# A fused linear-attention and SwiGLU kernel on one core: another order of work for its first five tiles

## The chip, the cores and the metric

The kernel runs on one core of a Trainium2 chip. The core has five engines that run side by side, each through its own list of instructions in order: TensorE (PE, matrix products; its weight loads are shown as PEld), VectorE (DVE), ScalarE (ACT), GpSimd (POOL) and SyncE (SP, which here only issues transfers). They wait for each other through semaphores. The metric is the device time of one execution in microseconds (us), the median over runs.

## The reference

One input x of 2048 rows and 512 columns is normalised and goes through linear attention with 32 heads of 16, and through a SwiGLU block with an inner width of 1792; both results are added to x. Weights and data are bfloat16.

```python
def _A_ref(x, wqkv, wo):
    qkv = (lambda x, *d: x.transpose(*d))((x @ wqkv).reshape(B, S, 3, H, Dh), 2, 0, 3, 1, 4)
    q, k, v = qkv[0], qkv[1], qkv[2]
    phi = lambda t: jnp.where(t > 0, t + 1, jnp.exp(t)) + 1e-6
    pq, pk = phi(q), phi(k)
    kv = jnp.einsum("bhsd,bhse->bhde", pk, v)
    z = jnp.einsum("bhsd->bhd", pk)
    num = jnp.einsum("bhqd,bhde->bhqe", pq, kv)
    den = jnp.einsum("bhqd,bhd->bhq", pq, z)[..., None] + 1e-6
    o = num / den
    return (lambda x, *d: x.transpose(*d))(o, 0, 2, 1, 3).reshape(B, S, D) @ wo

def _B_ref(x, w_gate, w_up, w_down):
    g = _silu(x @ w_gate)
    u = x @ w_up
    return (g * u) @ w_down

x = A_x
xn = _layernorm(x, axis=-1)
return x + _A_ref(xn, A_wqkv, A_wo) + _B_ref(xn, B_w_gate, B_w_up, B_w_down)
```

## The kernel before

The 2048 rows are 16 tiles of 128. Phase 1 runs over the tiles: layernorm, the products K = xn wk and Q = xn wq, the feature map phi, and a running product GT = xn^T phi(K), which stays in four PSUM banks (4 to 7) over all tiles (`gtacc`, line 516). V is never formed: after the last tile GT is multiplied by the V weights, masked per head and multiplied by wo. Phase 2 is the SwiGLU block, 56 steps of a gate product and an up product (`ffn`, line 692), with the attention's division and the output tiles placed between its steps. Only phase 1 is touched.

The order is written out by hand. A small recorder (`_Prog`) appends each operation to the list of its engine and derives the waits from the tiles that it reads and writes; what stands first in the text stands first on its engine. An operation that waits holds up everything behind it on that engine. Nothing is reordered later.

The steps of a tile t, with the names used below:

- `bns` (line 295) and `agg` (298), on VectorE: mean and variance. `rstd_pow` (313): variance plus 1e-5, on GpSimd or, for tiles 3 and 5, on VectorE, then the power -0.5 on GpSimd, which gives rstd.
- Tiles 0, 1 and 2 take a short way that doesn't wait for rstd: `xc_half` (346, VectorE) subtracts the mean in two halves, `tp_first` (356) transposes a half on PE (line 361) into bank 4 to 7 and copies it to SBUF on ScalarE (370), `proj_first` (395) multiplies two of the four blocks (half h) by the K or Q weights (line 400). rstd enters afterwards as the scale of ScalarE's `first_ek`, `first_pk`, `first_eq`, `first_pq` (exp of K, the positive part of K, exp of Q, Q).
- From tile 3 on: `xn_dve` (301, VectorE) writes the normalised tile, `transpose_dma` (374) issues a DMA transpose of it on SP's queue (line 377) into xnT, `kproj` and `qproj` (415, 418; matmuls at line 386) multiply it, `exp_k` and `exp_q` (421, 427) run on ScalarE; `exp_q` also copies Q.
- Features of K: `clip` (437, VectorE: min with 1, plus 1e-6), then `maxadd` (446) or, for tiles 1 and 2, `first_feat` (486) on VectorE; for tile 0 `feat_pool` (479) on GpSimd. The result is pk. `zsum` (504, GpSimd) adds pk up for the denominator; `feat_k` (493) bundles clip, the zsum of three tiles before, and maxadd.
- `gtacc(t)` needs xn and pk of the tile.

K of tile t goes to bank 2 (t mod 2), Q to the bank after it, so tile t + 2 waits until ScalarE and VectorE have read tile t's. At the start `fill` (264) runs matmuls on constants into bank 3.

Loads are issued first: x of tiles 0 to 5 one by one, the K weights and the Q weights in blocks, on SP's and ScalarE's queues; then x of tiles 6 to 9 and 10 to 13 on SP's queue. x of tiles 14 and 15 is loaded from ScalarE's queue, at the place in ScalarE's order where line 605 stands. Behind the loads SP's queue holds the DMA transposes in the order of the text. From t = 4 the loop at line 637 takes over; the dictionaries `STAT`, `XN0` and `XN` (632 to 635) say in which step the statistics and the normalisation of a later tile are done.

On PE the order of the groups before is: 8 long fills; transposes of tile 0 with 2 and 3 short fills behind its halves; K 0 first half; transposes of tile 1; K 0 second half; K 1; first halves of Q 0 and Q 1; transposes of tile 2; second halves of Q 0 and Q 1; K 2; GT 0; Q 2; GT 1; GT 2; K 3; Q 3; then K 4, Q 4, GT 3, K 5, and so on.

Of the kernel before, what the change touches and what calls it, by code (L numbers as in the profile page):

```python
# [10 lines left out]
P = 128  # L11
# [97 lines left out]
def bass_parallel_sum__linear_attn_block__swiglu_ffn__prompt_kernel(  # L109
# [16 lines left out]
    with contextlib.ExitStack() as es:  # L126
# [61 lines left out]
        def bk(i):  # L188
            return ("bank", i)
# [118 lines left out]
                r=[("x", t), ("mv", t), ("rstd", t)], w=[("xn", t)],  # L308
            )

        VD = (3, 5)

        def rstd_pow(t):
            eng, h = ("dve", dve) if t in VD else ("pool", pool)
            K.op(
                eng,
                lambda: h.tensor_scalar(
                    out=vpe[:, t:t + 1], in0=mv[:, t, 1:2], scalar1=1e-5, scalar2=None, op0=ALU.add,
                ),
                r=[("mv", t)], w=[("vpe", t)],  # L320
            )
            K.op(
                "pool",
                lambda: pool.tensor_tensor(out=rstd[:, t:t + 1], in0=vpe[:, t:t + 1], in1=nhalf[:, :], op=ALU.pow),
                r=[("vpe", t), ("nhalf",)], w=[("rstd", t)],
            )
# [82 lines left out]
        def kb(t):  # L409
            return 2 * (t % 2)  # L410
# [16 lines left out]
        def exp_q(t):  # L427
            K.op(
                "act", lambda: act.activation(eq[:, t, :], banks[qb(t)], ACT.Exp),
                r=[bk(qb(t))], w=[("eq", t)],  # L430
            )
            K.op(
                "act", lambda: act.activation(pkq[:, t, 1, :], banks[qb(t)], ACT.Copy),
                r=[bk(qb(t))], w=[("pq", t)],
            )

        def clip(e, res):
            K.op(
                "dve",
                lambda: dve.tensor_scalar(  # L440
                    out=e, in0=e, scalar1=1.0, scalar2=1e-6, op0=ALU.min, op1=ALU.add,
                ),
                r=[res], w=[res],
            )

        def maxadd(dst, src, e, r, w):
            K.op(
                "dve",
                lambda: dve.scalar_tensor_tensor(  # L449
                    out=dst, in0=src, scalar=0.0, in1=e, op0=ALU.max, op1=ALU.add,  # L450
                ),
                r=r, w=w,
            )
# [32 lines left out]
        def first_feat(t):  # L486
# [3 lines left out]
                r=[("kpos", t), ("ek", t)], w=[("pk", t)],  # L490
            )

        def feat_k(t):
            e = t % NE
            clip(ek[:, e, :], ("ek", e))
            if t >= 3:
                zsum(t - 3, e)
            maxadd(pkq[:, t, 0, :], banks[kb(t)], ek[:, e, :], [bk(kb(t)), ("ek", e)], [("pk", t)])

        def feat_q(t):  # L500
            clip(eq[:, t, :], ("eq", t))
# [2 lines left out]
        def zsum(t, e):  # L504
            pk = pkq[:, t, 0, :]
            after = [] if e is None else [("ek", e)]
            if t == 0:
                K.op("pool", lambda: pool.tensor_copy(zacc[:, :], pk), r=[("pk", t)] + after, w=[("zacc",)])
            else:
                K.op(  # L510
                    "pool",
                    lambda: pool.tensor_tensor(out=zacc[:, :], in0=zacc[:, :], in1=pk, op=ALU.add),  # L512
                    r=[("pk", t), ("zacc",)] + after, w=[("zacc",)],
                )
# [14 lines left out]
        def stat(t):  # L529
            bns(t)  # L530
            agg(t)
            rstd_pow(t)

        def xn(t):
            xn_dve(t)
            if t >= 3:
                transpose_dma(t)

        bns(0)
        agg(0)  # L540
        rstd_pow(0)
        xc_half(0, 0)
        xc_half(0, 1)
        bns(1)
        agg(1)
        rstd_pow(1)
        xc_half(1, 0)
        xc_half(1, 1)
        bns(2)
        agg(2)  # L550
        rstd_pow(2)
        xn_dve(0)
        xc_half(2, 0)
        xc_half(2, 1)

        fill(8, 512)
        tp_first(0, 0, 4)
        fill(2, P)
        tp_first(0, 1, 5)
        fill(3, P)  # L560
        proj_first(0, "wk", 0)
        tp_first(1, 0, 6)
        tp_first(1, 1, 7)
        proj_first(0, "wk", 1)
        first_ek(0)
        first_pk(0)
        proj_first(1, "wk", 0)
        proj_first(1, "wk", 1)
        first_ek(1)
        proj_first(0, "wq", 0)  # L570
        proj_first(1, "wq", 0)
        tp_first(2, 0, 4)
        tp_first(2, 1, 5)
        proj_first(0, "wq", 1)
        proj_first(1, "wq", 1)
        clip(ek[:, 0, :], ("ek", 0))
        feat_pool(0)
        bns(3)
        agg(3)
        rstd_pow(3)  # L580
        bns(4)
        clip(ek[:, 1, :], ("ek", 1))
        first_pk(1)
        first_eq(0)
        first_pq(0)
        proj_first(2, "wk", 0)
        proj_first(2, "wk", 1)
        gtacc(0)
        xn_dve(2)
        xn(3)  # L590
        agg(4)
        first_feat(1)
        rstd_pow(4)
        xn_dve(1)
        first_ek(2)
        first_pk(2)
        first_eq(1)
        first_pq(1)
        clip(ek[:, 2, :], ("ek", 2))
        xn(4)  # L600
        proj_first(2, "wq", 0)
        proj_first(2, "wq", 1)
        gtacc(1)
        first_eq(2)
        xload("act", act, 14, 2)
        first_pq(2)
        first_feat(2)
        bns(5)
        agg(5)
        rstd_pow(5)  # L610
        gtacc(2)
        bns(6)
        agg(6)
        rstd_pow(6)
        xn(5)
        kproj(3)
        exp_k(3)
        qproj(3)
        exp_q(3)
        bns(7)  # L620
        clip(ek[:, 0, :], ("ek", 0))
        xn(6)
        agg(7)
        rstd_pow(7)
        zsum(0, 0)
        maxadd(pkq[:, 3, 0, :], banks[kb(3)], ek[:, 0, :], [bk(kb(3)), ("ek", 0)], [("pk", 3)])
        bns(8)
        xn(7)
        agg(8)
        rstd_pow(8)  # L630

        STAT = {4: (9,), 5: (10,), 6: (11,), 7: (12,), 8: (13, 14), 9: (15,)}
        XN0 = {5: (8,), 6: (9,), 7: (10,), 8: (11,), 9: (12, 13), 10: (14,)}
        XN1 = {}
        XN = {10: (15,)}

        for t in range(4, NT):
            kproj(t)
            exp_k(t)
            qproj(t)  # L640
            exp_q(t)
            for i in XN0.get(t, ()):
                xn(i)
            feat_k(t)
            for i in XN1.get(t, ()):
                xn(i)
            for i in STAT.get(t, ()):
                stat(i)
            for i in XN.get(t, ()):
                xn(i)  # L650
            if t in (7, 8, 9):
                transpose_dma(t - 7)
            if t == 10:
                whalf("wg", wg_sb, B_w_gate, 0)
                whalf("wu", wu_sb, B_w_up, 0)
                wqkv_load("sp", sp, "wv", 2, 0, 4)
                wload("sp", sp, "wo", wo_sb, A_wo)
                whalf("wg", wg_sb, B_w_gate, 1)
            if t == 12:
                masks()  # L660
            if t >= 12:
                gtacc(t - 2)
            elif t < 11:
                gtacc(t - 1)
# [298 lines left out]
```

## Time and profile before

| what | value |
|---|---|
| median of 3 runs | 211.75 us (211.73 to 212.23) |
| span of the profiled execution, first to last instruction | 210.8 us |
| granted TensorE clock | 1.000 |
| DMA moved | 16.71 MB |
| HBM read, written | 9.70 MB, 2.10 MB |

The times of the profile lie inside the span and are counted from its first instruction; the median of the runs also has what lies around it. In the timeline a line gives the start, the length from the first start to the last end, the engine, the source line, the operation and its tiles, a count, and in brackets the idle time before it with what ended it. Matmuls overlap, so the lengths of neighbouring groups overlap as well; the distance of their starts is the measure. The lists of groups by line show these mean durations, which the prediction uses: 0.69 us for `bns` (line 296), 0.18 for `agg` (299), 0.48 for `xn_dve` (304), 0.28 for an `xc_half` (349), 0.69 for `maxadd` from PSUM (449), 0.67 for `first_feat` (489), 0.28 to 0.29 for `clip` (440), 0.60 for exp of K (423) and of Q (429), 0.70 for `first_ek` (457), 0.61 for the power on GpSimd (324), 1.15 for an addition on GpSimd (482 and 512).

### The profile page before, as it was taken

Reading aid. Unit: us, or ns where it says so; the run is one execution under the profiler, and the core shown is the slowest. Engines: PE = TensorE matmul, PEld = TensorE weight load, DVE = VectorE, ACT = ScalarE, POOL = GpSimd, SP = SyncE. Lnnn points to the kernel's source line nnn. Section 1 sums busy time; section 2 is a strip of 40 time slices with the busy share of each in tenths; the row PEclk is TensorE's granted clock in tenths of the full one; section 3 lists DMA queues with packets and bytes.
Section 4 is the critical chain, followed back from the end, with each engine's and each line's share of the span. In section 5 each row is a group of like instructions: output and inputs, shape, how many; then the busy total and the mean of one; then the engine's idle time right before and its main releaser. Section 6 shows DMA issues by size and latency. Waiting matters only on the chain.

```text
span 210.8 us, 2758 instructions
## 1 busy us (share of the span) xinstructions
PE 206.5 (98%) x972; PEld 95.8 (45%) x991; DVE 119.7 (57%) x245; ACT 69.8 (33%) x122; POOL 74.4 (35%) x95
## 2 busy tenths in 40 slices
PE   8999999999999999999999999999999999999996
PEld 3444444445444444444444444444444444444455
DVE  4899889335364775546274746365556535374121
ACT  3797666666543331203122312213031213121000
POOL 3647987659032444222140432230424132221200
DMA  6773244794793011110101110102021010110201
GB/s 205 228 214 78 51 100 101 219 369 167 197 357 67 0 26 27 46 25 28 50 2 50 24 28 25 50 0 50 3 50 25 25 25 30 49 27 25 51 28 50
DMA packets 29455, 16.71 MB, mean 79 GB/s; under 512 B 20224, under 2 KB 29056, under 8 KB 29440
## 3 DMA queue, kind: packets, MB, share of 16 engines
q1 hardware_dynamic: 28304, 15.34, 26.4%
q10 hardware_dynamic: 1136, 1.18, 1.8%
q8 instruction: 8, 0.13, 0.2%
q14 instruction: 7, 0.06, 0.1%
HBM read 9.70 MB, written 2.10 MB: 56 GB/s over the span
## 4 chain that ended last, share of the span: by engine, by line
PE 95%; DMA 3%; issue 1%; ACTq 0%; ACT 0%; DVE 0%
PE psum L683 46%; PE psum L866 23%; PE psum L386 11%; PE psum L520 7%; PE psum L855 7%; DMA wqkv_sb<-in_A_wqkv_dram 3%; PE psum L400 2%; PE psum L781 0%; PE psum L804 0%; ACT L232 0%; ACTq L209 0%; DVE out_sb L879 0%; ACTq L202 0%; PE psum L361 0%
## 5 line engine op out<-in xcount | busy, mean ns | idle before, releaser
L698 ACT ACTIVATE sg<-psum 128x512 bf16<-128x512 f32 x56 | 33.4, 598 | 106.8 <-PE psum L683 106.0
L683 PE MATMUL psum<-xnT,wu_sb 128*128 128x512 bf16 x222 | 57.4, 379 | 0.1
L683 PE MATMUL psum<-xnT,wg_sb 128*128 128x512 bf16 x217 | 56.0, 379 | 0.4
L813 POOL TENSOR_TENSOR prod<-pkq,zb 128x512 f32<-128x512 bf16 x16 | 18.6, 1160 | 57.9 <-DVE pkq L449 57.9
L683 PEld LDWEIGHTS psum<-xnT,wu_sb 128*128 128x128 bf16 x224 | 21.9, 98 | 26.4
L683 PEld LDWEIGHTS psum<-xnT,wg_sb 128*128 128x128 bf16 x224 | 21.9, 98 | 26.2
L879 DVE TENSOR_TENSOR out_sb<-psum,x_sb 128x512 bf16<-128x512 f32 (+1 forms) x17 | 11.2, 660 | 35.6 <-PE psum L866 35.6
L837 POOL TENSOR_TENSOR pqn<-pkq,rden 128x512 bf16<-128x512 bf16 x16 | 16.9, 1055 | 36.5 <-DVE rden L831 36.5
L704 DVE TENSOR_TENSOR pkq<-psum,sg 128x512 bf16<-128x512 f32 x28 | 19.1, 687 | 18.6 <-PE psum L683 14.1
L704 DVE TENSOR_TENSOR xn_sb<-psum,sg 128x512 bf16<-128x512 f32 x28 | 18.8, 671 | 14.5 <-PE psum L683 13.0
L866 PE MATMUL psum<-wd_sb,xn_sb 128*128 128x512 bf16 (+1 forms) x124 | 25.6, 355 | 0.1
L866 PE MATMUL psum<-wd_sb,pkq 128*128 128x512 bf16 x110 | 25.4, 379 | 0.1
L386 PE MATMUL psum<-wqkv_sb,xnT 128*128 128x512 bf16 x102 | 24.2, 379 | 0.1
L512 POOL TENSOR_TENSOR zacc<-zacc,pkq 128x512 f32<-128x512 f32 x15 | 17.3, 1154 | 5.0 <-DVE ek L440 4.6
L866 PEld LDWEIGHTS psum<-wd_sb,xn_sb 128*128 128x128 bf16 x126 | 12.3, 98 | 11.9
L866 PEld LDWEIGHTS psum<-wd_sb,pkq 128*128 128x128 bf16 x112 | 11.0, 98 | 13.2
L855 PE MATMUL psum<-m_sb,eq 128*128 128x512 bf16 (+1 forms) x66 | 16.2, 366 | 0.1
L520 PE MATMUL psum<-pkq,xn_sb 128*128 128x512 bf16 x63 | 15.8, 379 | 0.1
L386 PEld LDWEIGHTS psum<-wqkv_sb,xnT 128*128 128x128 bf16 x104 | 10.1, 98 | 12.4 <-DMA xnT<-xn_sb 0.4
L821 DVE TENSOR_REDUCE den<-prod 128x32 f32<-128x512 f32 x16 | 10.9, 684 | 5.9 <-POOL prod L813 5.9
L296 DVE BATCH_NORM_STATS2 stats<-x_sb 128x6 f32<-128x512 bf16 x16 | 11.0, 685 | 3.6 <-DMA x_sb<-in_A_x_dram 3.6
L449 DVE SCALAR_TENSOR_TENSOR pkq<-pkq,eq 128x512 bf16<-128x512 bf16 x16 | 11.1, 692 | 0.6
(59 smaller groups left out, 139.0 us busy)
## 6 DMA issues: line engine op xcount, KB each, us to landing
out_dram<-out_sb SPq DMA_DIRECT2D x15, 128.0 KB, 1.7
wg_sb<-in_B_w_gate_dram SPq DMA_DIRECT2D x2, 896.0 KB, 8.2
wu_sb<-in_B_w_up_dram SPq DMA_DIRECT2D x2, 896.0 KB, 5.9
wd_sb<-in_B_w_down_dram SPq DMA_DIRECT2D x1, 1792.0 KB, 9.8
x_sb<-in_A_x_dram SPq DMA_DIRECT2D x2, 512.0 KB, 3.9
x_sb<-in_A_x_dram SPq DMA_DIRECT2D x4, 128.0 KB, 4.1
wqkv_sb<-in_A_wqkv_dram SPq DMA_DIRECT2D x1, 512.0 KB, 7.7
wo_sb<-in_A_wo_dram SPq DMA_DIRECT2D x1, 512.0 KB, 10.1
```

Source lines behind the costliest of these rows:

```text
L386: (lambda c=c: pe.matmul(banks[b], xnT[:, c, t * P:(t + 1) * P], wqkv_sb[:, c, lo:lo + D], start=(c == 0), stop=(c == NDC - 1),))
L449: lambda: dve.scalar_tensor_tensor(out=dst, in0=src, scalar=0.0, in1=e, op0=ALU.max, op1=ALU.add,),
L512: lambda: pool.tensor_tensor(out=zacc[:, :], in0=zacc[:, :], in1=pk, op=ALU.add),
L520: (lambda c=c: pe.matmul(banks[4 + c], xn_sb[:, t, c * P:(c + 1) * P], pkq[:, t, 0, :], start=(t == 0), stop=(t == NT - 1),))
L683: (lambda c=c: pe.matmul(banks[b], w_sb[:, c, fc * P:(fc + 1) * P], xnT[:, c, C * 512:(C + 1) * 512], start=(c == 0), stop=(c == NDC - 1),))
L698: lambda: act.activation(sg[:, j % NSG, :], banks[gb], ACT.Silu),
L704: lambda: dve.tensor_tensor(out=hT(C, fc), in0=banks[ub], in1=sg[:, j % NSG, :], op=ALU.mult,),
L813: lambda: pool.tensor_tensor(out=p, in0=pkq[:, t, 1, :], in1=zb[:, :], op=ALU.mult),
L837: lambda: pool.tensor_tensor(out=pqn[:, t % NPN, :].rearrange("p (h e) -> p h e", e=DH), in0=pkq[:, t, 1, :].rearrange("p (h e) -> p h e", ...
L855: (lambda g=g: pe.matmul(dst, pqnT(t)[:, g, :], m_sb[:, g, lo:hi], start=(g == 0), stop=False,))
L866: (lambda fc=fc: pe.matmul(dst, hT(C, fc)[:, jj * P:(jj + 1) * P], wd_sb[:, fc, lo:hi], start=False, stop=(fc == NFC - 1),))
L879: lambda: dve.tensor_tensor(out=o, in0=src, in1=x_sb[:, t, lo:hi], op=ALU.add),
```

## The change

The operations are the same, and so are their number, their engines and the loads ahead; their order in the text changes, and with it the order on each engine. `rstd_pow` is split into `eps` (variance plus 1e-5, its engine now an argument) and `rstd_of` (the power), `exp_q` into `exp_q` and `copy_q`, and `feat_k` into `clip_k` and `maxadd_k`, so that they can be placed apart. The 2 and 3 short fills become 5 behind both halves of tile 0's transposes.

On PE the order is now: 8 long fills; transposes of tile 0; 5 short fills; K 0 first half; transposes of tile 1; K 0 second half; K 1; **transposes of tile 2**; first halves of Q 0, Q 1 **and K 2**; second halves of Q 0, Q 1 and K 2; GT 0; Q 2; GT 1; **Q 3; K 3; GT 2**; K 4; Q 4; GT 3; K 5, and so on. On VectorE tile 2's halves of xc stand ahead of xn of tiles 0 and 1, and xn 3 ahead of the statistics of tile 4 and of xn 2. On GpSimd the rstd of tile 2 moves behind that of tile 3. On ScalarE the copies of tile 2's transposes stand ahead of the exp of K 1, and the features of Q 0 and Q 1 in another order; Q 2's copy stands behind the exp of K 3. The statistics of tile 9 move from step 4 to step 5 (together with those of tile 10), and the normalisation and DMA transpose of tile 7 from the hand-written part to step 5, that of tile 8 to the end of step 5.

```diff
-        def rstd_pow(t):
-            eng, h = ("dve", dve) if t in VD else ("pool", pool)
+        def eps(t, eng):
+            h = dve if eng == "dve" else pool
...
+        def rstd_of(t):
...
         bns(0)
+        fill(8, 512)
         agg(0)
-        rstd_pow(0)
+        eps(0, "pool")
+        rstd_of(0)
         xc_half(0, 0)
+        tp_first(0, 0, 4)
         xc_half(0, 1)
+        tp_first(0, 1, 5)
+        fill(5, P)
+        proj_first(0, "wk", 0)
         bns(1)
         agg(1)
-        rstd_pow(1)
         xc_half(1, 0)
+        tp_first(1, 0, 6)
+        eps(1, "pool")
         xc_half(1, 1)
...
         tp_first(1, 1, 7)
         proj_first(0, "wk", 1)
         first_ek(0)
         first_pk(0)
         proj_first(1, "wk", 0)
         proj_first(1, "wk", 1)
-        first_ek(1)
+        bns(2)
+        agg(2)
+        xc_half(2, 0)
+        tp_first(2, 0, 4)
+        xc_half(2, 1)
+        tp_first(2, 1, 5)
         proj_first(0, "wq", 0)
         proj_first(1, "wq", 0)
-        tp_first(2, 0, 4)
-        tp_first(2, 1, 5)
+        proj_first(2, "wk", 0)
+        rstd_of(1)
+        xn_dve(1)
+        first_ek(1)
+        first_pk(1)
         proj_first(0, "wq", 1)
+        first_pq(0)
+        first_eq(0)
         proj_first(1, "wq", 1)
-        clip(ek[:, 0, :], ("ek", 0))
+        first_eq(1)
+        proj_first(2, "wk", 1)
+        clip_k(0)
         feat_pool(0)
         bns(3)
         agg(3)
-        rstd_pow(3)
+        eps(3, "dve")
+        rstd_of(3)
+        xn_dve(0)
+        gtacc(0)
+        clip_k(1)
+        first_pq(1)
+        proj_first(2, "wq", 0)
+        proj_first(2, "wq", 1)
+        xn_dve(3)
         bns(4)
...
         agg(4)
         first_feat(1)
-        rstd_pow(4)
-        xn_dve(1)
+        gtacc(1)
+        eps(2, "pool")
+        rstd_of(2)
         first_ek(2)
         first_pk(2)
...
+        xn_dve(2)
         first_eq(2)
         xload("act", act, 14, 2)
+        transpose_dma(3)
+        qproj(3)
+        exp_q(3)
+        copy_q(3)
+        kproj(3)
+        exp_k(3)
+        eps(4, "pool")
+        rstd_of(4)
+        xn(4)
         first_pq(2)
-        first_feat(2)
         bns(5)
         agg(5)
-        rstd_pow(5)
+        eps(5, "dve")
+        rstd_of(5)
+        clip_k(2)
+        first_feat(2)
         gtacc(2)
...
         xn(5)
-        kproj(3)
-        exp_k(3)
-        qproj(3)
-        exp_q(3)
...
+        stat(6)
+        kproj(4)
+        clip_k(3)
+        zsum(0, 0)
+        maxadd_k(3)
+        exp_k(4)
+        qproj(4)
         xn(6)
...
+        exp_q(4)
+        copy_q(4)
+        clip_k(4)
+        zsum(1, 1)
+        stat(7)
+        maxadd_k(4)
+        stat(8)
+        gtacc(3)
+
+        STAT = {5: (9, 10), 6: (11,), 7: (12,), 8: (13, 14), 9: (15,)}
+        XN0 = {5: (7,), 6: (9,), 7: (10,), 8: (11,), 9: (12, 13), 10: (14,)}
         XN1 = {}
-        XN = {10: (15,)}
-
-        for t in range(4, NT):
+        XN = {5: (8,), 10: (15,)}
+
+        for t in range(5, NT):
```

## The prediction

> **What bounds the kernel now.** I read the page first: is one engine full, and where is it not?
>
> ```profile
> span 210.8 us, 2758 instructions
> PE 206.5 (98%) x972; PEld 95.8 (45%) x991; DVE 119.7 (57%) x245; ACT 69.8 (33%) x122; POOL 74.4 (35%) x95
> ...
> PE   8999999999999999999999999999999999999996
> ```
>
> TensorE is busy 98% of the span; the first slice and the last are the only ones that aren't full. So a reordering of the first five tiles can only win back idle time of PE in the first slices, or make new idle time. Next I read the chain of waits: one line of it (start, length), a weight load, precedes a run of matmuls that lasts to the end.
>
> ```profile
> 2.40 5.32 DMA wqkv_sb<-in_A_wqkv_dram
> ```
>
> Then PE's timeline from 0 to 20 us (start, length, engine, line, operation, count):
>
> ```profile
> 5.90 1.56 PE L400 MATMUL psum<-wqkv_sb,xcT 128*128 128x512 bf16 x6
> 7.86 1.02 PE L400 MATMUL psum<-wqkv_sb,xcT 128*128 128x512 bf16 x4 [0.39 <-DMA wqkv_sb<-in_A_wqkv_dram]
> 8.72 0.39 PE L361 MATMUL psum<-ident,xc_sb 128*128 128x128 bf16 x4
> 8.94 1.89 PE L400 MATMUL psum<-wqkv_sb,xcT 128*128 128x512 bf16 x8
> 10.67 1.03 PE L520 MATMUL psum<-pkq,xn_sb 128*128 128x512 bf16 x4
> ...
> 12.40 2.02 PE L520 MATMUL psum<-pkq,xn_sb 128*128 128x512 bf16 x8
> 14.25 3.66 PE L386 MATMUL psum<-wqkv_sb,xnT 128*128 128x512 bf16 x16
> ```
>
> The chain has 16 matmuls in 3.45 us, so a 512-column matmul steps by 0.216 us, and four by 0.863; starts count, since lengths overlap. Last, the weight loads of PE (PEld) at the places where a start is late, from narrow windows of the timeline:
>
> ```profile
> 6.42 0.11 PEld L400 LDWEIGHTS psum<-wqkv_sb,xcT 128*128 128x128 bf16 x2 [0.42 <-ACT xcT L370]
> ...
> 13.37 0.11 PEld L520 LDWEIGHTS psum<-pkq,xn_sb 128*128 128x128 bf16 x2 [0.44 <-DVE pkq L489]
> ...
> 16.00 0.11 PEld L386 LDWEIGHTS psum<-wqkv_sb,xnT 128*128 128x128 bf16 x2 [0.36 <-DMA xnT<-xn_sb]
> ```
>
> PE's own holes: six matmuls from 5.90 should end at 7.20, the hole before 6.42 makes it 7.30 (0.10); the next starts at 7.86 (**0.56**, the second block of the Q weights, issued 2.40, landed 7.72); GT 1's four from 12.40 end at 13.26, GT 2's start at 13.37 (**0.11**); K 3 and Q 3, eight from 14.25, end at 15.97, K 4 starts at 16.01 (0.04, tile 4's transpose). They sum to 0.81 us, and behind 16.01 I find none: proj, GT and FFN matmuls start 0.216 apart. So **no version of this order can win more than 0.8 us of 210.8, 0.38%**.
>
> **The change, part by part.** No instruction is added or removed; fills of 2 and 3 become one of 5, and 0.107 us each at the half-rate start is the same sum. All loads of the first 12 us are issued in the same order on the same queues, so I take the same landings. Up to 7.30 us PE's order gives the same starts.
>
> Tile 2's transposes (L361) go ahead of Q 0. They need xc of tile 2, which loses xn 0 in front of it on VectorE: agg 2 starts at 6.63, and agg 1 at 5.01 had its xc at 5.23, so the halves start at 6.85 and 7.05 and end (0.28 each) by 7.33. The four transposes, 8.72 to 8.94 before (0.22), now run from 7.30 to 7.53, inside the 0.56 hole. Q 0 still waits for its weights until 7.86: **-0.22**. ScalarE copies them at 7.69 and 7.97 behind kpos 0, done 8.35. Then Q 0, Q 1 halves to 8.72, K 2's first half to 9.15 (its bank is free: kpos 0 ended 7.80), Q 0, Q 1 second halves to 10.01, K 2's to 10.45. GT 0 at 10.45 instead of 10.67 needs pk 0 of GpSimd (clip 0 ends 7.82, kpos 0 7.80, so 7.9 + 1.15 = 9.05) and xn 0 (about 9.35): both early. Q 2 at 11.31 needs its bank: pq 0 waits for Q 0's end (9.37 + 0.38 = 9.75), then eq 0 ends 11.05. Cover 0.26 us. GT 1 at 12.17 needs pk 1: exp 1 now stands behind the copies, 8.23 to 8.92; clip 1 9.25, xn 3 9.66, bns 4, agg 4, then first_feat 1 at 10.83 to 11.49. Cover 0.7. GT 1 ends at **13.03** against 13.26.
>
> Then Q 3 and K 3 instead of GT 2. The **0.11** hole is gone, since GT 2, now at 14.8 or later, has its pk 2 at about 14.3 (kpos 2 ends 13.35, clip 2, add 0.68). But Q 3 now needs tile 3's DMA transpose (L377) 1.2 us sooner than K 3 did at 14.25, and that one is the crux. The queue of SP and its landings, with ACT's last x load:
>
> ```profile
> 7.91 0.81 SPq L202 DMA_DIRECT2D x_sb<-in_A_x_dram  x2
> 10.81 3.12 SPq L377 DMA_TRANSPOSE xnT<-xn_sb  x2
> ...
> x_sb<-in_A_x_dram SPq DMA_DIRECT2D x2, 512.0 KB, 3.9
> x_sb<-in_A_x_dram ACTq DMA_DIRECT2D x1, 256.0 KB, 2.8
> xnT<-xn_sb SPq DMA_TRANSPOSE x1, 2.5
> xnT<-xn_sb SPq DMA_TRANSPOSE x1, 3.2
> xnT<-xn_sb SPq DMA_TRANSPOSE x1, 2.4
> ```
>
> The transposes in these lines are those of tiles 3, 4 and 5. Tile 3's was issued at 10.81 and landed at 13.34. It goes out when xn 3 is ready. xn 3's rstd comes from GpSimd right behind pk 0 (9.06 to 9.61), xn 2 and bns 4 no longer stand before it, so xn 3 is 9.66 to 10.06 and the issue 10.1, 0.7 sooner. If the landing follows, it comes at 10.1 + 2.4 = 12.5 and Q 3 doesn't wait. But in front of it on SP's queue stands the load of x 10 to 13: issued 8.28, landed 12.7 (the two loads take 3.4 and 4.4, median 3.9). Tile 4's transpose shows what a load in flight does to one: issued at 12.75 behind ACT's load of 12.60, it took 3.2 instead of 2.4. The last data of x 10 to 13 go at about 12.3; behind them the transpose's own data (0.75 on every tile) and the landing end near 13.3 whether it is issued at 10.1 or 10.8. Bounds: 12.5 and 13.34. I take 13.30, by tile 4's row. One sentence of the Trainium skill bears on it, page "DMA: Bandwidth & Descriptors", section "Queues, rings and completion order": on each DMA engine the descriptors of one queue are consumed in ring order; by it the sum goes by 13.3 and not 12.5.
>
> So Q 3 starts at 13.35 instead of 13.03: **+0.32**. Twelve matmuls (Q 3, K 3, GT 2) later, 13.35 + 2.59 = **15.94**, K 4 starts, against 16.01. Its transpose: rstd 2 and rstd 4 end about 10.65 and 11.9, xn 4 12.0 to 12.4, issue 12.45; ACT's load goes out when Q 2 ends (11.95 + 0.38), 12.37. Both are 0.25 to 0.3 ahead of before and in the same order, so it lands near 15.7: cover 0.2. Q 4's bank waits for pq 2, now behind exp 3 on ScalarE: about 15.4 + 0.49 + 0.73 = 16.6 at the latest, and Q 4 comes at 16.80. Cover 0.2.
>
> Behind that the statistics and transposes of tiles 7 and 8 are later than before. VectorE: exp 3 ends 15.95, then clip 3, maxadd 3, xn 6 (16.9), clip 4, bns 7, maxadd 4, bns 8, agg 8 by 20.1, xn 7 at 20.0 to 20.5: transpose 7 issued 20.55 against 18.63, landed 22.96, and K 7 is wanted at 15.94 + 3 x 2.59 = 23.71. clip 5 20.4, maxadd 5, bns 9, agg 9, bns 10, agg 10 (22.97), xn 8 at 23.07 to 23.5: transpose 8 issued 23.5 against 20.96, landed 25.9; K 8 is wanted at 26.30. Cover 0.35 us, where it had nearly 3. Tile 9's xn follows at once, its transpose waits on SP's queue for tile 8's (1.3), lands 27.4, wanted 28.9. From there it is the old pattern.
>
> Sum at K 4: -0.22 - 0.11 - 0.04 + 0.32 and rounding = **-0.07 us** of the profiled 210.84; nothing behind K 4 changes. The median of the runs, 211.75, is 0.9 above the span; I carry that over: **211.68 us**. Bounds: with the landing at 12.5, K 4 is held by its own transpose at 15.75 (-0.26) or, if that too comes 0.3 sooner, by PE at 15.62 (-0.39).
>
> **The rivals.** (1) *Tile 3's transpose isn't held by the loads*: Q 3 at 13.03, gain 0.26 to 0.39, 211.4 to 211.5. For it: the engines that finish x 10 to 13 first can start on it. Against it: a landing needs the last engine. (2) *The change buys nothing or a little less*: the wait of GT 2 only moves to Q 3 and then to K 4. If ACT's x load goes out a little further ahead of transpose 4 and that one lands at 16.3, K 4 starts at 16.36: net +0.35, 212.1. (3) *Slower: transpose 8.* Two statistics and two xn now lie in tile 5's step, and the point of decision is an issue of transpose 8 later than 23.8. VectorE's xn shows how it can come:
>
> ```profile
> 18.02 0.58 DVE L304 TENSOR_SCALAR xn_sb<-x_sb,mv,rstd 128x512 bf16<-128x512 bf16 x1
> 19.62 1.15 POOL L512 TENSOR_TENSOR zacc<-zacc,pkq 128x512 f32<-128x512 f32 x1
> 20.33 0.60 DVE L304 TENSOR_SCALAR xn_sb<-x_sb,mv,rstd 128x512 bf16<-128x512 bf16 x1
> ```
>
> An xn that meets a zacc operation of GpSimd takes 0.58 to 0.60 instead of 0.38, and ends just after it. If the zacc of tile 2 (which I have at 21.1 to 22.3) slid under xn 8, xn 8 would end up to 0.9 later, issue 24.4, landing 26.8 (2.41) to 27.2 (2.77, as tile 9's took), K 8 late by 0.55 to 0.9: net +0.5 to +0.85, 212.2 to 212.6. The Trainium skill, "SBUF — State Buffer", section "SBUF: two separate sides", calls the port that VectorE and GpSimd share an exclusive lock under which the loser blocks for the other's whole instruction; the two ends seen here agree. (4) *Faster by over 0.3%* would need 0.64 of the 0.81 us, though 0.34 of the weight wait and the 0.10 remain: only run-to-run difference gives it.
>
> **How the numbers follow.** Forecast 0.48; rival 1 0.24; rival 2 0.14; rival 3 0.10; rival 4 0.04. A difference under 0.3%, 0.64 us, is about what a measurement of this kernel can't tell from no change. The forecast, rival 1 and rival 2 fall inside it (0.86, of which I give 0.03 to slower for stalls that add up); rival 3 mostly outside. Faster 0.04, same 0.83, slower 0.13. The likeliest case's own range is 211.5 to 211.9; the range reaches over rival 1 and the near end of rival 3: 211.3 to 212.2.
>
> **What would show it.** In the changed profile: the L361 group of tile 2 at 7.30, Q 0 still at 7.86; GT 0 near 10.45; transpose 3 issued near 10.1 but landing near 13.3, and PEld of Q 3 waiting for xnT until 13.3; K 4 near 15.94; transposes 7 and 8 near 20.5 and 23.5 with no hole of PE at K 7 and K 8. It is wrong if the Q weights land at another time, if Q 3 waits past 13.7, or if a hole opens between 16 and 30 us.

## The result, and the profile after

The changed kernel takes 213.05 us, median of six runs (212.82 to 214.27), against 211.90 us (211.73 to 212.28) for the kernel before in the same session: 1.0059 times [1.0041, 1.0077]. Eleven more runs of it in a second session gave 212.71 us against 212.14, 1.0030 [1.0019, 1.0040]. It is slower, by 0.3 to 0.6%; 211.68 was predicted.

The profiled execution of the first session took 214.27 us, the longest of its six, and is not typical. From its page:

```profile
span 213.0 us, 2756 instructions
...
PE 207.2 (97%) x972; PEld 95.7 (45%) x991; DVE 120.2 (56%) x245; ACT 69.8 (33%) x122; POOL 73.9 (35%) x95
...
PE   8999979999999999999999999999999999999996
```

PE's work is the same; the 7 in the sixth slice (26.6 to 32.0 us) is new idle time. The timeline of PE of the same execution (start, length, engine, line, operation, count, idle time before it):

```profile
7.88 0.48 PE L361 MATMUL psum<-ident,xc_sb 128*128 128x128 bf16 x4
8.20 2.75 PE L400 MATMUL psum<-wqkv_sb,xcT 128*128 128x512 bf16 x12
...
13.60 1.89 PE L386 MATMUL psum<-wqkv_sb,xnT 128*128 128x512 bf16 x8
15.58 1.04 PE L527 MATMUL psum<-pkq,xn_sb 128*128 128x512 bf16 x4
16.46 1.89 PE L386 MATMUL psum<-wqkv_sb,xnT 128*128 128x512 bf16 x8
...
25.95 1.03 PE L527 MATMUL psum<-pkq,xn_sb 128*128 128x512 bf16 x4
28.58 1.67 PE L386 MATMUL psum<-wqkv_sb,xnT 128*128 128x512 bf16 x7 [1.60 <-DMA xnT<-xn_sb]
```

The last line is K 8, waiting for tile 8's DMA transpose. GT 6 starts at 25.95, so K 8 was due at 26.81 and the hole, the idle time of PE, is 1.77 us. K 4 starts at 16.46, 0.45 later than in the profile of before. The two make 2.2, which is the difference of the spans (213.0 and 210.8): in every profile of this study the first FFN matmul starts 21.6 us after K 8, and the span ends 162.9 us after that in these executions, so **all of the loss is made before K 8**.

The second session's profile (span 211.5, time 212.71, its median) is the typical one. Its PE timeline at the same places:

```profile
7.33 0.39 PE L361 MATMUL psum<-ident,xc_sb 128*128 128x128 bf16 x4
7.78 2.75 PE L400 MATMUL psum<-wqkv_sb,xcT 128*128 128x512 bf16 x12
...
13.48 1.89 PE L386 MATMUL psum<-wqkv_sb,xnT 128*128 128x512 bf16 x8 [0.37 <-DMA xnT<-xn_sb]
15.21 1.03 PE L527 MATMUL psum<-pkq,xn_sb 128*128 128x512 bf16 x4
16.07 1.89 PE L386 MATMUL psum<-wqkv_sb,xnT 128*128 128x512 bf16 x8
...
25.57 1.03 PE L527 MATMUL psum<-pkq,xn_sb 128*128 128x512 bf16 x4
27.01 1.89 PE L386 MATMUL psum<-wqkv_sb,xnT 128*128 128x512 bf16 x8 [0.42 <-DMA xnT<-xn_sb]
```

K 4 comes at 16.07 and K 8's hole is 0.58 (27.01 against 25.57 + 0.86). The kernel before, profiled in that session (211.70 us, span 210.5), has K 4 at 15.64 and K 8 at 26.00. So 0.43 and 0.58 make the 1.01 us between these two executions: not quite half of the loss is made before K 4.

The cause of the hole at K 8 is in the list of DMA issues, in a window that holds only tile 8's transpose (count, us from issue to landing). The kernel before in the second session:

```profile
xnT<-xn_sb SPq DMA_TRANSPOSE x1, 2.4
```

The changed kernel in the second session:

```profile
xnT<-xn_sb SPq DMA_TRANSPOSE x1, 3.4
```

The changed kernel in the first session:

```profile
xnT<-xn_sb SPq DMA_TRANSPOSE x1, 4.5
```

It is issued at 23.51 and 23.93 in the changed kernel (20.63 before), and takes 1 to 2 us more to land. What is in flight beside it shows in the list of DMA queues (packets, MB, share), here the 0.4 us from 25.2 to 25.6 of the changed kernel in the second session:

```profile
q1 hardware_dynamic: 131, 0.03, 33.0%
q14 instruction: 1, 0.01, 5.9%
```

and 24 to 26 us of the changed kernel in the first session:

```profile
q8 instruction: 1, 0.02, 4.4%
q14 instruction: 1, 0.01, 3.4%
```

By their kind, "instruction", I take these packets of 8 KB (q14) and 16 KB (q8) for an engine's code being fetched. With the 8 KB one in its flight the transpose took 3.4 us, with both 4.5, and SP's own issue instruction 2.43 instead of 1.19. The 8 KB fetch belongs to a place in the program: it comes at 24.0 to 24.1 us in the kernel before and at 24.7 to 26.3 in the changed one and its variants, and in 17 of the 18 profiles VectorE has then started 53 or 54 of its operations. So VectorE's order moves the fetch as well as the transpose. Before, it fell into the flight of tile 9's transpose (2.8 and 3.1 us, with some 3 us to spare); now it falls into tile 8's.

The Trainium skill, "Runtime: NRT & Kernel Launch", section "Instruction fetch mechanics", says that each engine's instruction memory is refilled in 16 KiB blocks through a DMA queue and that the cost is mostly hidden. These traces have blocks of 8 KB too. What a fetch costs the engine that fetches, no run here shows; for a DMA transpose in flight beside it the cost was not hidden: 1.0 and 2.1 us.

The slipped landing is half of it. The other half is that the transpose is issued 2.9 us later, and that is VectorE's order. Most of it is the place of xn 8, behind the statistics of tiles 9 and 10: before_late8 below, with that place in the kernel before, issues it at 23.80. The rest is time that VectorE loses. Busy time of VectorE in stretches of 2 us (stretch, its length, busy, operations, clock, DMA share, GB/s), the kernel before in the second session:

```profile
12.00:14.00 2.00, 1.93 (x6) 1.00 0.53 128
14.00:16.00 2.00, 1.92 (x5) 1.00 0.41 101
16.00:18.00 2.00, 1.90 (x5) 1.00 0.46 93
```

and the changed kernel there:

```profile
12.00:14.00 2.00, 1.48 (x5) 1.00 0.60 131
14.00:16.00 2.00, 1.86 (x5) 1.00 0.52 152
16.00:18.00 2.00, 1.69 (x5) 1.00 0.33 66
```

Before, VectorE is full from 12 to 24 us (11.5 of 12.0 over all six stretches; 10.8 in the changed kernel). The 0.7 us that it waited more are work that comes later. The largest piece, in VectorE's timeline of the changed kernel, is xn 4 waiting for rstd 4:

```profile
12.45 0.41 DVE L304 TENSOR_SCALAR xn_sb<-x_sb,mv,rstd 128x512 bf16<-128x512 bf16 x1 [0.54 <-POOL rstd L324]
```

GpSimd itself had waited for agg 4, which VectorE has at 10.83, behind xn 3 and bns 4:

```profile
11.10 0.57 POOL L315 TENSOR_SCALAR vpe<-mv 128x1 f32<-128x1 f32 x1 [0.48 <-DVE mv L299]
11.75 0.58 POOL L324 TENSOR_TENSOR rstd<-vpe,nhalf 128x1 f32<-128x1 f32 x1
```

In the kernel before rstd 4 is no sooner (11.61 to 12.20 in its first profile), but there clip 2 stands ahead of xn 4.

### The profile page after: what moved, and what is told of

Its sections match the earlier page's. It is cut to its first block, busy times and chain, and to the rows that moved or that the text cites. A ratio compares the mean times of both kernels' runs of the same rounds, so it can differ in the third digit from the quotient of the medians.

```text
span 213.0 us, 2756 instructions
## 1 busy us (share of the span) xinstructions
PE 207.2 (97%) x972; PEld 95.7 (45%) x991; DVE 120.2 (56%) x245; ACT 69.8 (33%) x122; POOL 73.9 (35%) x95
## 4 chain that ended last, share of the span: by engine, by line
PE 85%; DVE 5%; DMA 4%; POOL 3%; issue 1%; ACT 0%; ACTq 0%; DVEq 0%; POOLq 0%
PE psum L700 45%; PE psum L883 23%; PE psum L386 7%; PE psum L872 6%; PE psum L527 4%; DMA x_sb<-in_A_x_dram 2%; DMA xnT<-xn_sb 2%; DVE stats L296 2%; POOL rstd L324 1%; DVE xn_sb L304 1%; POOL vpe L315 1%; POOL pkq L484 1%; DVE mv L299 1%; POOL zacc L519 1%; PE psum L798 0%
## 5 line engine op out<-in xcount | busy, mean ns | idle before, releaser
L883 PE MATMUL psum<-wd_sb,xn_sb 128*128 128x512 bf16 (+1 forms) x124 | 25.6, 355 | 0.1
L883 PEld LDWEIGHTS psum<-wd_sb,xn_sb 128*128 128x128 bf16 x126 | 12.3, 98 | 11.9
```

What stands on the lines that cost most here:

```text
L883: (lambda fc=fc: pe.matmul(dst, hT(C, fc)[:, jj * P:(jj + 1) * P], wd_sb[:, fc, lo:hi], start=False, stop=(fc == NFC - 1),))
```

## The experiments

Ratios are to the kernel before on the same chip. Diffs are against the changed kernel unless said otherwise. Each variant has one profile, and executions of one kernel differ by up to a microsecond, so a hole seen in a profile and a median of several runs need not tell the same.

**Both kernels again** (after_again and before_again), unchanged: above.

> The changed kernel once more, for a second profile and more times. Theory A (tile 8's DMA transpose, issued near 23.9 us instead of 21.0, lands after K 8 wants it): a hole of PE of 0.4 us or more right before K 8 in this profile too, 26.4 us or later, and a median of 212.8 to 213.3. Rival B (the loss is made ahead of K 4, by tile 2's transposes waiting for the load of x 2 and by Q 3 waiting for tile 3's transpose): no hole at K 8, and K 4 starts at 16.8 or later. Rival C (an instruction fetch met tile 8's transpose by chance, as the 16 KB packet at 24.5 us of the first profile suggests): no hole at K 8 and a median under 212.3.

> The kernel before once more, for a second profile: how far the landings of the first loads and the places of the instruction fetches differ from one execution to the next. All theories: PE without a hole of over 0.2 us behind 13.4 us, 211.7 to 212.3. If x 2 lands anywhere from 5.9 to 6.6 us here and PE still starts K 4 near 16.0, its order hides that landing; rival B then has its cause.

Theory A's hole came (0.58, at 27.01), with a median just under its range. Rival C is out; rival B is not, for part of the loss: K 4 comes later than before, though not at 16.8. In the kernel before x of tile 2 landed at 5.47, and PE had no hole behind 13.4.

**xn8_first**: tile 8's normalisation and transpose ahead of the statistics of tiles 9 and 10.

```diff
-        XN1 = {}
-        XN = {5: (8,), 10: (15,)}
+        XN1 = {5: (8,)}
+        XN = {10: (15,)}
```

> The changed kernel with the normalisation and transpose of tile 8 ahead of the statistics of tiles 9 and 10 in step 5; nothing else. Its issue should come 1.5 us sooner, near 22.4. Theory A: no hole at K 8 and 0.8 to 1.4 us faster than the changed kernel, 211.6 to 212.2. Rival B: under 0.3 us faster, 212.7 or more. Rival C: as fast as the changed kernel is where no fetch meets the transpose.

212.62 us, 1.0029 [1.0015, 1.0042]. Tile 8's transpose was issued at 22.80, landed after 2.4 us, and K 8's hole was gone; in its place PE waited 0.45 us ahead of GT 6, for a feature product of VectorE:

```profile
25.99 1.04 PE L527 MATMUL psum<-pkq,xn_sb 128*128 128x512 bf16 x4 [0.28 <-DVE pkq L451]
```

Where VectorE lost it shows in its timeline in the same profile:

```profile
21.54 1.24 DVE L304 TENSOR_SCALAR xn_sb<-x_sb,mv,rstd 128x512 bf16<-128x512 bf16 x1
```

and in GpSimd's:

```profile
21.47 1.15 POOL L519 TENSOR_TENSOR zacc<-zacc,pkq 128x512 f32<-128x512 f32 x1
```

xn 8 started beside the zacc operation and took 1.24 us instead of 0.41: the meeting that the prediction's rival 3 described, here at 0.83 us. So removing the named wait gave back nothing measurable: theory A, tile 8's transpose alone, misses its 211.6 to 212.2.

**tp2_back**: tile 2's transposes and K 2 back behind Q 0 and Q 1, the rest as changed.

```diff
-        tp_first(2, 0, 4)
...
-        tp_first(2, 1, 5)
         proj_first(0, "wq", 0)
         proj_first(1, "wq", 0)
-        proj_first(2, "wk", 0)
...
+        tp_first(2, 0, 4)
+        tp_first(2, 1, 5)
...
+        proj_first(2, "wk", 0)
```

> The changed kernel with tile 2's transposes and K 2's first half behind the first halves of Q 0 and Q 1 again, exp of K 1 ahead of their copies as before; the rest as changed. Theory A: the hole at K 8 stays, 212.6 to 213.4, at most 0.3 us from the changed kernel. Rival B: 0.4 us or more faster than the changed kernel, and K 4 starts before 16.1.

212.90 us, 1.0040 [1.0026, 1.0054], with the hole at K 8 (0.60; transpose 3.4 us). K 4 came at 16.25, no sooner. Part 1 is not what costs.

**xn89**: as xn8_first, and xn 9 behind the features of tile 6.

```diff
-        XN0 = {5: (7,), 6: (9,), 7: (10,), 8: (11,), 9: (12, 13), 10: (14,)}
-        XN1 = {}
-        XN = {5: (8,), 10: (15,)}
+        XN0 = {5: (7,), 7: (10,), 8: (11,), 9: (12, 13), 10: (14,)}
+        XN1 = {5: (8,), 6: (9,)}
+        XN = {10: (15,)}
```

> The changed kernel with xn 8 ahead of the statistics of tiles 9 and 10, and xn 9 behind the features of tile 6. Theory A2 (from K 4 to K 8 the loss is one of order on VectorE: work of tiles 8 to 10 that is wanted late stands in the same queue with work that is wanted now): PE has no hole between K 4 and K 9, K 8 starts 10.35 us behind K 4, and the median is 0.4 to 0.6 us under the changed kernel's of the last call, 212.0 to 212.3. Rival D (VectorE simply has too much work there, so that a hole only moves): a hole of 0.4 us or more remains at one of K 8, GT 6, GT 7, 212.5 or more.

212.71 us, 1.0035 [1.0022, 1.0047]. No hole at K 8 nor at GT 6, but 0.55 at K 6: tile 6's transpose took 3.7 us with the 16 KB fetch in its flight, which came at 18.85 in this execution. That fetch comes elsewhere in others, so this hole does not speak for rival D; the median, in its range, does.

**bns5_first**: statistics of tile 5 ahead of xn 4, into VectorE's wait.

```diff
+        bns(5)
         xn(4)
...
-        bns(5)
```

> The changed kernel with the statistics of tile 5 (bns) ahead of xn 4, in the 0.54 us in which VectorE waited for rstd 4; nothing else. Theory A2: tile 8's transpose is issued 0.3 to 0.5 us sooner, near 23.1, and the hole at K 8 shrinks by as much, to under 0.3 us: 212.2 to 212.5. Rival D gives the same. Rival C (the hole is the instruction fetch that met the transpose): the hole is 0.5 us or more wherever a packet of 8 or 16 KB lies between the issue of transpose 8 and its landing, whatever the issue, and 0 otherwise.

212.90 us, 1.0046 [1.0032, 1.0061]: a miss. The wait for rstd 4 went, and VectorE waited 0.33 and 0.46 ahead of clip 3 and clip 4 instead; K 8's hole stayed (0.58).

**before_late8**: the kernel before, with only statistics 9 in step 5 and xn 8 behind statistics 9 and 10.

```diff
-        STAT = {4: (9,), 5: (10,), 6: (11,), 7: (12,), 8: (13, 14), 9: (15,)}
-        XN0 = {5: (8,), 6: (9,), 7: (10,), 8: (11,), 9: (12, 13), 10: (14,)}
+        STAT = {5: (9, 10), 6: (11,), 7: (12,), 8: (13, 14), 9: (15,)}
+        XN0 = {6: (9,), 7: (10,), 8: (11,), 9: (12, 13), 10: (14,)}
...
-        XN = {10: (15,)}
+        XN = {5: (8,), 10: (15,)}
```

> The kernel before with one part of the change alone: statistics of tile 9 in step 5 with those of tile 10, and xn 8 and its transpose behind them. Theory A2: the transpose is issued near 22.9 instead of 20.6 and K 8 is wanted near 26.0 to 26.4, so it still lands in time without a fetch (25.3) and up to 0.3 us late with one: 0 to 0.3 us slower than before. Rival D: 0.5 us or more slower. If it is as slow as the changed kernel, the whole loss is this one part.

212.58 us, 1.0026 [1.0016, 1.0036]. The transpose was issued at 23.80 and took 3.1 us with the 8 KB fetch at 25.00; K 8 came at 27.03 behind a hole of 0.49. The late place of transpose 8 alone, on the old order of PE, makes the hole, and the median, 0.60 above that of the kernel before, is as slow as the changed kernel's: theory A2's 0 to 0.3 is missed. The profile (212.81) is slower than the median, and half a microsecond of it is another thing: a hole of 0.83 ahead of GT 2, which waits for pk 2 at a place that the edit does not touch.

**x10_behind_t3**: the changed kernel with the load of x 10 to 13 issued behind tile 3's transpose on SP's queue.

```diff
-        xload("sp", sp, 10, 4)
...
         transpose_dma(3)
+        xload("sp", sp, 10, 4)
```

> The changed kernel with the load of x 10 to 13 behind tile 3's transpose on SP's queue instead of ahead of it. If that load holds the transpose, as the prediction has it, the transpose lands 2.4 to 2.6 us behind its issue, near 12.7, and Q 3's hole of 0.2 to 0.5 us is gone; tile 4's transpose then waits behind the load, lands at 16.0 or later, and K 4 starts no sooner than 16.0. If something else holds it, it lands near 13.3 as before. The time is open: 212.3 to 213.3.

214.38 us, 1.0118 [1.0090, 1.0146]. Tile 3's transpose took 2.5 us and landed at 13.08, Q 3's hole was 0.14; tile 4's took 3.6 (issued 13.24, behind the load), and K 4 was late by 0.84. A load ahead of a transpose on the queue does hold it; the cost only changed tiles. The median lies above the range expected, and 0.84 is half of what it lost against the changed kernel; the rest is open, since the profiled execution (213.76) is among the fastest of the six.

**tail_old**: the changed order up to GT 2, then the statistics, normalisations and transposes of tiles 6 to 10 as in the kernel before.

```diff
+        bns(6)
+        agg(6)
...
-        stat(6)
...
-        STAT = {5: (9, 10), 6: (11,), 7: (12,), 8: (13, 14), 9: (15,)}
-        XN0 = {5: (7,), 6: (9,), 7: (10,), 8: (11,), 9: (12, 13), 10: (14,)}
+        STAT = {5: (10,), 6: (11,), 7: (12,), 8: (13, 14), 9: (15,)}
+        XN0 = {5: (8,), 6: (9,), 7: (10,), 8: (11,), 9: (12, 13), 10: (14,)}
...
-        XN = {5: (8,), 10: (15,)}
+        XN = {10: (15,)}
```

> The changed kernel up to GT 2, and from there the order of the kernel before for the statistics, normalisations and transposes of tiles 5 to 10. Theory A3 (from K 4 to K 8 the changed order leaves the transposes of tiles 6 to 8 under 1.2 us between landing and use, and an instruction fetch that comes in their flight adds 0.4 to 2 us to one of them; the order before leaves 1.9 to 3 us): no hole of PE between K 4 and K 9, and a median 0.4 to 0.7 us under the changed kernel's, at most 0.4 us above before, 211.8 to 212.4. Rival B (the first part costs as much by itself): 0.5 us or more above before, with no hole behind K 4. Rival D: a hole of 0.4 us or more remains.

212.78 us, 1.0034 [1.0022, 1.0047]. No hole at K 8 (transpose 8 issued 21.67, landed 24.26), but 0.48 ahead of GT 3:

```profile
18.28 1.04 PE L527 MATMUL psum<-pkq,xn_sb 128*128 128x512 bf16 x4 [0.32 <-DVE pkq L451]
```

Theory A3 is out. With the old order of the later work, VectorE's lateness comes due at GT 3, 8.7 us ahead of K 8. The deficit is made ahead of that, in the first four tiles.

**tail_old_x6 and before_x6**: tail_old and the kernel before, with the loads of x 6 to 13 issued behind x 2 instead of x 3.

```diff
-        xload("sp", sp, 6, 4, [("x", 3)])
+        xload("sp", sp, 6, 4, [("x", 2)])
```

> As tail_old, with the loads of x 6 to 13 let go when x 2 has landed and not x 3, 1.3 to 2 us sooner. If that load holds tile 3's transpose, the transpose lands 2.4 to 2.5 us behind its issue, near 12.8, K 4 starts near 15.7, and the kernel is 0.1 to 0.4 us faster than tail_old; if the earlier load takes the DMA engines from the Q weights, Q 0 starts later than 8.2 and it is slower.

> The kernel before with the same earlier loads of x 6 to 13, as the measure for tail_old_x6. K 3 stands behind GT 2 here, so tile 3's transpose has 0.9 us to spare: no gain from its landing; tile 4's, which K 4 waits for by 0.04 to 0.1 us, may come 0.1 us sooner: -0.1 to +0.1 us.

212.71 us, 1.0035 [1.0016, 1.0054], and 212.08 us, 0.9999 [0.9987, 1.0012]. The loads were issued 1.7 to 2 us sooner (5.92 against 7.87, 5.65 against 7.34 in before_again) but landed little or no sooner: x 10 to 13 at 12.77 against 12.66, and at 12.06 against 12.28. So the edit did not bring them forward, and whether their landing limits is not shown by it.

**before_part1**: the kernel before with tile 2's transposes and the first half of K 2 ahead, GT 2 staying ahead of K 3. **pe_only**: the same, and K 3 and Q 3 ahead of GT 2, so PE's order is that of the change (but K 3 stands ahead of Q 3, and the short fills are 2 and 3 as before), while VectorE, GpSimd and SP keep theirs save for one exchange of xn 0. Their core, against the kernel before:

```diff
+        tp_first(2, 0, 4)
+        tp_first(2, 1, 5)
...
-        tp_first(2, 0, 4)
-        tp_first(2, 1, 5)
+        proj_first(2, "wk", 0)
...
-        proj_first(2, "wk", 0)
...
-        gtacc(2)
...
+        gtacc(2)
```

> The kernel before with the first part of the change alone: tile 2's xc ahead of xn 0, its transposes ahead of Q 0 and Q 1, K 2's first half between their halves; GT 2 stays ahead of K 3. By the prediction GT 1 ends 0.2 us sooner, and GT 2, which waits for pk 2, eats what is won: -0.2 to +0.1 us, 211.8 to 212.2. Rival B: 0.3 us or more slower, since PE now waits for x 2 where Q 0 and Q 1 could have gone first.

> The kernel before with the changed order of PE alone: tile 2's transposes and K 2's first half ahead (as before_part1), and K 3 and Q 3 ahead of GT 2; VectorE, GpSimd and SP keep the order before from tile 3 on. Rival D: the order of PE costs nothing by itself, the loss came with VectorE's order: no hole at K 8 or GT 3, GT 2's wait of 0.1 to 0.3 us gone, a wait of up to 0.4 us at K 3 for transpose 3: 211.5 to 212.1, not slower than before by more than 0.2 us. Rival B (PE's order is the cost): 0.4 us or more above before.

before_part1: 211.89 us, 0.9989 [0.9976, 1.0001]; pe_only: 212.08 us, 1.0002 [0.9992, 1.0013]. **PE's new order costs nothing.** In pe_only tile 8's transpose is issued at 20.61 and takes 2.4 us, K 4 comes at 15.76 and K 8 at 26.13, and VectorE's windows are those of the kernel before:

```profile
12.00:14.00 2.00, 1.93 (x6) 1.00 0.45 80
14.00:16.00 2.00, 1.90 (x6) 1.00 0.54 157
16.00:18.00 2.00, 1.92 (x5) 1.00 0.47 95
```

before_part1 is the best version seen, but its interval reaches 1: no gain that this measurement can tell.

**half_stats**: the changed kernel with the statistics of tiles 9 and 10 over half of the columns; it leaves out half of that work, and its statistics there are not those of the tile.

```diff
-            K.op("dve", lambda: dve.bn_stats(stats[:, t, :], x_sb[:, t, :]), r=[("x", t)], w=[("st", t)])
+            n = HD if t in (9, 10) else D
+            K.op("dve", lambda: dve.bn_stats(stats[:, t, :], x_sb[:, t, 0:n]), r=[("x", t)], w=[("st", t)])
```

> The changed kernel with the statistics of tiles 9 and 10 taken over the first 256 columns alone: it leaves out half of two bn_stats, 0.34 us each of VectorE's work in step 5, and keeps every order. Rival D as the runs so far leave it (VectorE is late by what it lost ahead of K 4, and the loss shows as a hole of PE wherever its lateness is paid): transpose 8 is issued 0.6 to 0.7 us sooner, near 22.9, lands before K 8 wants it even if the 8 KB fetch comes at 25.4, and the kernel is 0.4 to 0.6 us faster than the changed one, 212.0 to 212.3. Theory C (the fetch alone): the landing stays at 26.8 or later, and the time too.

No hole of PE behind K 4: K 8 at 26.39, though its transpose still took 3.3 us, because it was issued 0.5 sooner. In these two executions the hole needs both, the late issue and the slow landing. The profiled execution took 212.18 us, but the median of twelve is 212.52, 1.0030 [1.0014, 1.0045]: the profile shows the hole gone, the median does not show the loss gone.

**before_extra**: the kernel before with one more `bns` of tile 5, 0.69 us of VectorE.

```diff
+        bns(5)
```

> The kernel before with one more bn_stats of tile 5 (its result is written twice): 0.69 us of VectorE's time at about 13 us, nothing else. Rival D: VectorE has 0.2 to 0.4 us to spare at GT 3, so 0.3 to 0.5 us come out as a hole of PE at GT 3 or K 4, 212.3 to 212.6. If VectorE isn't what limits this stretch: no hole, 211.8 to 212.1.

212.51 us, 1.0030 [1.0019, 1.0040], and a hole of 0.54 at the place where tail_old had its own:

```profile
18.17 1.04 PE L520 MATMUL psum<-pkq,xn_sb 128*128 128x512 bf16 x4 [0.38 <-DVE pkq L449]
```

VectorE, which the page shows 57% busy, has almost nothing to spare in this stage: 0.69 us of it cost 0.4 to 0.6 us of the kernel (the medians differ by 0.44, and 0.3% of 212 is 0.64).

**dve_fill**: statistics of tiles 5 to 9 placed ahead of each operation of VectorE that waited, xn 7 ahead of the statistics of tile 9, xn 8 and xn 9 as in xn89.

```diff
+        bns(5)
...
+        stat(6)
...
+        stat(7)
...
+        stat(8)
...
+        xn(7)
+        stat(9)
...
-        XN = {5: (8,), 10: (15,)}
+        XN = {10: (15,)}
```

> The changed order of PE with VectorE's waits filled: the statistics of tiles 5 to 9 stand in front of the operations that wait for ScalarE or GpSimd (xn 4, clip 2, clip 3, clip 4, clip 5), xn 8 ahead of the statistics of tile 10, xn 9 behind the features of tile 6. Rival D: transposes 7 and 8 are issued 1 to 2 us sooner than in the changed kernel, no hole of PE from K 4 to K 9 with or without a fetch, 211.8 to 212.3. If a hole of 0.4 us stays, the lost VectorE time isn't the cause.

212.62 us, 1.0039 [1.0017, 1.0061]: a miss as a repair. K 8's hole was 0.07, with its transpose at 3.3 us, but GT 2 had one of 0.34, waiting for pk 2, which now stood behind a statistic.

## Why the prediction was wrong

- **The bound** was right: PE's work did not change (206.5 us busy before and 207.2 after, each with 19 matmul records missing, and 207.2 and 207.7 in the second session), and the whole difference is holes before K 8.
- **Part 1**, -0.22, depended on "I take the same landings", and that does not hold from one execution to the next. x of tile 2 landed at 5.88 in the profile of before and at 6.56 in the changed one of the first session, where tile 2's transposes came at 7.88 instead of 7.30 and held back Q 0. In before_again the Q weights landed at 7.11 and PE had no hole there, so nothing was to be won.
- **The sum at K 4**, -0.07, failed too. K 4 was predicted at 15.94; it came at 16.46 and 16.07, and in the kernel before at 16.01 and 15.64. Over the profiles it comes at 15.64 to 16.18 in the seven with the old order on VectorE (median 15.81) and at 16.02 to 16.59 in the ten with the changed head (median 16.1; x10_behind_t3 left aside): about 0.3 us later. In the pair of the second session the 0.43 is 0.19 from the Q weights, which landed later in that execution (7.64), and 0.25 because Q 3 now waits 0.53 for its transpose where GT 2 had waited 0.28 for pk 2. In pe_only, with the same groups on PE, the wait for tile 3's transpose was 0.07. In the changed kernel there rstd 4, predicted at about 11.9, came at 12.33, and tile 4's transpose was issued at 12.89 instead of 12.45.
- **Q 3 and tile 3's transpose**, the step called the crux, was right: landing predicted 13.30, measured 13.35 and 13.46; Q 3 predicted 13.35, measured 13.48 and 13.60. In all 17 profiles with the load of x 10 to 13 ahead of it, this transpose landed within 0.1 us of the later of two times: 2.53 behind its issue, or 0.6 behind the landing of that load. In the second session it was the load (12.76 + 0.6), as predicted; in the first, by luck near the same time, the late issue (10.88 + 2.53). x10_behind_t3 showed the hold on tile 4's. Rival 1 is out.
- **GT 2's hole** was counted as gone (-0.11). It was gone in the second session (15.21, eight matmuls behind Q 3) but 0.26 in the first.
- **The failed step** is "transpose 8 issued 23.5 against 20.96, landed 25.9; K 8 is wanted at 26.30. Cover 0.35 us". Its first half was exact (xn 8 predicted 23.07, measured 23.10; issue 23.51). The term that was mis-sized is the flight of the transpose: 2.41 us by the kernel before's row, it took 3.37 and 4.5, with the code fetch in it, so the cover of 0.35 became a hole of 0.58 and 1.77. With 2.41 it would have landed at 25.92 and left no hole. The kernel before's own trace had the row: tile 9's transpose with 2.77, the only one in flight at that 8 KB fetch. The prediction had that 2.77 as a bound for rival 3, and did not ask what made it.
- **Rival 3**, slower through transpose 8, had the place and the order of size, at a chance of 0.10, but another mechanism: xn 8 beside GpSimd's zacc. In the changed kernel they do not meet; in xn8_first they do, at 0.83 us.
- **What the prediction did not ask**: it followed a chain of single operations, each with its own cover, and had VectorE's times at tile 8 right by it; it did not add up VectorE's work over the stage, which tells how little room any order leaves. Any of xn8_first, tail_old, xn89 and dve_fill closes the hole at K 8 (to 0.07 at most) and stays 0.3 to 0.4% slow, with a later K 4 and a hole elsewhere; before_extra makes such a hole by adding work; pe_only, which leaves VectorE's order alone from tile 3 on, loses nothing; before_late8, which changes only VectorE's order (and with it that of GpSimd's and SP's work for tiles 8 and 9), loses as much as the changed kernel. These show that PE's order does not make the loss and that VectorE's can. Not shown: which of VectorE's, GpSimd's and ScalarE's new orders makes the head late, since no run separates them there, and how much of the loss is lateness and how much the fetch, since half_stats closed the hole without bringing the median back.
- **The time beside the span**, carried over as 0.9, is 1.2 to 1.4 in every run that gives both (211.70 and 210.5; 212.71 and 211.5), so the profile of before was of a slower execution than its median. It cancels in the forecast, which is the median before less 0.07, and explains nothing of the miss.

## What to carry to other kernels

Where two engines are full in a stage, count both: an order that moves a wait off the engine that sets the time is paid for in the other's waits, and a late engine shows up at whatever comes due next, so that removing the named hole only moves it. Read the busy time by stage and not over the span: VectorE is 57% busy over this kernel and 96% from 12 to 24 us, and what it loses there can come back as idle time of PE (before_extra: 0.69 us of work, a hole of 0.54). A DMA's flight time should be taken at the slowest row of its kind, with what flew beside it, before a cover of a few tenths is called enough.

## What the runs showed of the hardware

- A DMA transpose with a packet of the kind "instruction" in its flight lands later. Tile 8's took 2.4 us without one, 3.1 to 3.4 with the 8 KB one, 4.2 to 4.5 with both; with the 16 KB one alone tile 6's took 3.7 in xn89 and a later tile's 4.1 in after_again. It matters when the fetch comes: the 8 KB one made the flight 2.7 to 3.1 us when it came 0.9 to 1.2 us behind the issue (tile 9's in the kernel before and its like) and 3.3 to 3.4 when it came 1.8 to 1.9 us behind it. One that came in the last 0.15 us (tile 7's in the profile of before) did nothing, and a 16 KB one that came 0.02 to 0.08 us ahead of the issue left 2.4 us in two profiles and made it 2.6 to 2.7 in four. This goes by rows of 18 profiles; no run takes the fetch away by itself, and how a fetch of one packet holds a landing is open.
- The 8 KB fetch keeps its place in the program (54 operations of VectorE started; in before_extra, with one operation more, it came at 22.17, with 49 started). The 16 KB one came anywhere from 18.85 to 28.48 us, at 20.91 and 25.15 in the two profiles of the kernel before, so the same kernel meets it at another transpose each time.
- First loads differ between executions by more than the head can win: the second block of the Q weights, issued at 2.40 in all, landed at 7.72 and 7.11 in the two profiles of the kernel before and from 6.65 to 7.72 over all 18.
- An xn of VectorE that starts beside an addition of GpSimd took 1.24 us instead of 0.41 and ended after it (22.78 and 22.62). The Trainium skill, "SBUF — State Buffer", section "SBUF: two separate sides", describes the port that the two engines share as an exclusive lock; this row agrees in that the xn ended only behind the addition.
